# Splitting a transposing DMA into four pieces, one for each pair of heads, in a fused attention and bilinear-FFN kernel

## The chip, the cores and the metric

The kernel runs on one core of one Trainium2 chip. Times are device microseconds for one execution of the whole program; the median of several runs is quoted. Ratios are the mean time of one kernel's fast runs over the mean of the other's fast runs that are listed with it, so they are not quite the ratio of the medians. (Of the six runs of the kernel before that the changed kernel is set against, three are those that were known when the prediction was made.) All runs quoted as ratios were fast, that is, none was more than 1.5% above the fastest run of its kernel.

One core has several engines that work side by side: TensorE (PE) for matmuls, VectorE (DVE), ScalarE (ACT), GpSimd (POOL) and SyncE (SP). In this kernel POOL issues the DMAs that load and cast inputs, and SP issues stores and the transposing DMAs. The profile counts the packets of all of them together, on the core's 16 DMA engines.

## The reference, cut to what matters

```python
# batch, n_heads, seq, head_dim = 8, 8, 576, 64; d_model 512, d_ff 1536, 4608 tokens
kv  = np.einsum('bhsd,bhse->bhde', k, v)
out = np.einsum('bhsd,bhde->bhse', q, kv)
rms = np.sqrt(np.mean(out * out, axis=-1, keepdims=True) + 1e-06)
x   = (out / rms * g_norm)            # then to (tokens, d_model)
y   = ((x @ w_a) * (x @ w_b)) @ w_out
```

Almost all of the arithmetic is in the three FFN products. Attention is done batch by batch, just ahead of the FFN blocks that use it. Its matmuls want q with head_dim on the partitions, that is, transposed.

## The kernel before

The program is laid out by a small list scheduler in the kernel's own Python. Each piece of work is a node with an engine, a believed duration, a priority and its dependencies, each with a believed latency in microseconds. `plan.order()` runs through believed time and emits the instructions in the order that results. The beliefs are not waits: on the chip each engine takes its instructions in that fixed order, and semaphores hold it where the data isn't there. A wrong belief gives no wrong result; it gives an order in which an engine stands still.

Batches 0 and 1 are transposed on TensorE. From the third batch on, q is cast to bf16 into a scratch in DRAM and read back by a transposing DMA:

```python
def load_node(b, prio, dep, xt=None):          # dep: the load of the batch before
    ...
    def issue():                                # on POOL
        if dep is not None:
            # the gate: one element of the batch before's transposed q, copied to hold POOL
            nc.gpsimd.tensor_copy(gate_t, dep["q"].tile[0:1, 0, 0:1])
        ...
        for hl in range(2):                     # q -> scratch, cast to bf16
            nc.gpsimd.dma_start(out=scr[:, :, hl, :].rearrange("p s d -> s p d"), in_=qv[hl])
        ...                                     # then k in five DMAs, v in two
    def transpose():                            # on SP
        nc.sync.dma_start_transpose(
            out=ld["q"].tile[:].rearrange("p a s -> p (a s)"),
            in_=scr[:].rearrange("a s h d -> (a s) (h d)"),
        )
    ...
    ld["n"]  = plan.add("POOL", issue_us, prio, issue, ([(dep["qn"], 8.0)] if dep else []) + ..., ...)
    ld["qn"] = plan.add("SP", 2.5, prio, transpose, [(ld["n"], q_us)], [ld["q"]])
```

The load of the output weights (`wo_t`) stands behind the same kind of gate, on batch 2's q, and ahead of batch 3's load:

```python
def load_wo(dep):
    def issue():
        nc.gpsimd.tensor_copy(gate_t, dep["q"].tile[0:1, 0, 0:1])
        for i in range(2):
            sl = slice(i * FC // 2, (i + 1) * FC // 2)
            nc.gpsimd.dma_start(out=wo_t[:, sl, :], in_=wo_v[:, sl, :])
    return plan.add("POOL", 1.8, 50.0, issue, [(dep["qn"], 8.0)])
```

The first block's output product (L943 in the profile) reads `wo_t`; the scheduler believes that its halves are there 5.8 and 10.6 us after that issue:

```python
# in o_std
n1 = plan.add("PE", mm_us(OP, d_model), pr + 0.01 * f0, mm,
     [(wo_n, 5.8 if f0 + OP <= FC // 2 else 10.6), n1] + ..., ...)
```

Lines to know in the profile: L839 and L1008 are the FFN products, L943 the first block's output product, L624 the k·v product of a batch, L353 and L539 the readers of transposed q, L701 and L656 the gates, L704 the load of wo.

## Time and profile before

| | before |
|---|---|
| median time, 6 runs | 297.49 us (296.86 to 298.25) |
| span of the profiled run | 294.8 us |
| TensorE busy | 288.1 us, 98% |
| batch 2's transpose: starts, issued in, landed | 41.98, 6.49, 51.88 us |
| gate opens, wo issued | 51.94, 52.56 and 53.38 us |
| wo halves landed | 60.67 and 64.66 us |
| first L943 | 60.94 us |

Most of the lines behind this table stand in the prediction below. The "chain" of a page is the work that ended last, followed back step by step to what released it; its shares say what each step was, not what it cost. Read a timeline row as start, duration, engine, line, operation, output and inputs, count. "SPq" and "POOLq" rows are queues of these engines.

### The profile page before, as it was taken

The page shows a single profiled execution, that of the slowest core. Times are in us where ns is not written, and L with a number is a line of the kernel's source. Part 1 is how long each engine was busy: PE and PEld are TensorE (multiplying, and loading weights), DVE is VectorE, ACT ScalarE, POOL GpSimd, SP SyncE. Part 2 cuts the span into 40 slices and gives each one's busy share as a digit, 9 for nine tenths or more (in the row PEclk, how much of TensorE's full clock was granted, in tenths as well). Part 3 has the DMA queues.
Part 4 walks back from the last instruction along what each step waited for, and adds up shares of the span by engine and source line. Part 5 has one row for each costly group of instructions (what it writes and reads, how often), then busy time and mean ns, then how long its engine had stood idle before and what let it go on. Part 6 is the DMA issues. An engine that isn't in the chain of part 4 may idle for free.

```text
span 294.8 us, 6757 instructions
## 1 busy us (share of the span) xinstructions
PE 288.1 (98%) x2646; PEld 238.1 (81%) x2648; DVE 240.2 (81%) x441; ACT 191.7 (65%) x395; POOL 77.1 (26%) x96
## 2 busy tenths in 40 slices
PE   8999999999999999999999999999999999999993
PEld 3645558965888988899988998898988888888882
DVE  5454879893987988789979999979989958788852
ACT  3757667876578677877757866786769546665420
POOL 8945830950092470380001910000000000000000
PEclk9999999999999999999999999999999999999999
DMA  8999999699999999499816999330155001200053
GB/s 181 198 199 200 196 158 166 102 168 183 189 128 171 143 170 173 48 136 210 174 31 149 145 166 167 80 145 21 38 85 165 2 0 43 102 2 0 9 172 107
DMA packets 112643, 36.26 MB, mean 123 GB/s; under 512 B 89060, under 2 KB 108516, under 8 KB 112612
## 3 DMA queue, kind: packets, MB, share of 16 engines
q0 software_dynamic: 77552, 18.44, 65.9%
q1 hardware_dynamic: 34448, 16.70, 26.8%
q10 hardware_dynamic: 612, 0.71, 0.8%
q8 instruction: 20, 0.33, 0.5%
q14 instruction: 11, 0.09, 0.1%
HBM read 37.75 MB, written 14.75 MB: 178 GB/s over the span
## 4 chain that ended last, share of the span: by engine, by line
PE 93%; DVE 4%; issue 1%; ACT 1%; DVEq 0%; ACTq 0%
PE bk L839 47%; PE bk L1008 24%; PE bk L387 7%; PE bk L310 3%; PE bk L943 3%; PE bk L624 2%; PE bk L353 2%; PE bk L367 2%; PE bk L341 1%; PE bk L539 1%; PE bk L325 1%; DVE c L858 1%; DVE so L746 1%; DVE o_sb L1046 1%; DVE T L806 1%
## 5 line engine op out<-in xcount | busy, mean ns | idle before, releaser
L858 DVE TENSOR_TENSOR c<-bk,u 128x512 f16<-128x512 f32 x144 | 96.1, 684 | 19.3 <-PE bk L839 11.8
L420 ACT COPY u<-bk 128x512 f32<-128x512 f32 x144 | 81.4, 591 | 36.5 <-PE bk L839 29.9
L839 PE MATMUL bk<-xp,wa_t 128*128 128x256 f16 x288 | 55.0, 273 | 0.1
L839 PE MATMUL bk<-xp,wb_t 128*128 128x256 f16 x288 | 55.0, 273 | 0.0
L839 PEld LDWEIGHTS <-wa_t 128*128 128x128 f16 x384 | 37.1, 98 | 5.7 <-issue 0.3
L1008 PEld LDWEIGHTS <-abt 128*128 128x128 f16 x384 | 37.5, 98 | 4.7 <-issue 0.3
L839 PEld LDWEIGHTS <-wb_t 128*128 128x128 f16 x384 | 37.6, 98 | 4.4
L1008 PE MATMUL bk<-wo_t,abt 128*128 128x256 f16 x288 | 37.2, 273 | 0.1
L839 PE MATMUL bk<-T,sb 128*128 128x256 f16 x192 | 36.7, 273 | 0.0
L839 PE MATMUL bk<-T,sa 128*128 128x256 f16 x192 | 36.7, 272 | 0.0
L420 ACT CAST c<-bk 128x512 f16<-128x512 f32 x48 | 28.0, 587 | 12.1 <-PE bk L839 11.5
L893 DVE TENSOR_TENSOR abt<-c 128x1024 f16<-128x1024 f16 x48 | 32.7, 684 | 0.9
L839 PEld LDWEIGHTS <-sb 128*128 128x128 f16 x288 | 28.2, 98 | 3.3
L839 PEld LDWEIGHTS <-sa 128*128 128x128 f16 x288 | 27.9, 98 | 3.5
L1008 PEld LDWEIGHTS <-as 128*128 128x128 f16 x288 | 28.1, 98 | 3.3
L1040 ACT COPY o_sb<-bk 128x512 f32<-128x512 f32 x31 | 18.2, 586 | 18.5 <-PE bk L1008 18.0
L376 DVE SCALAR_TENSOR_TENSOR xp<-bk,g_col,rs 128x288 f16<-128x288 f32 x40 | 20.2, 512 | 10.9 <-ACT rs L371 10.9
L1008 PE MATMUL bk<-so,as 128*128 128x256 f16 x192 | 25.2, 273 | 0.0
L371 ACT ACTIVATE rs<-bk,eps_t 128x288 f32<-128x288 f32 x40 | 20.0, 506 | 6.2 <-PE bk L367 6.1
L667 POOL DMA_DIRECT2D k_t<-in_k_dram x24 | 21.2, 899 | 0.8 <-issue 0.5
L661 POOL DMA_DIRECT2D scr<-in_q_dram x12 | 19.6, 1638 | 2.5 <-issue 1.5
L1046 DVE TENSOR_TENSOR o_sb<-bk,o_sb 128x512 f32<-128x512 f32 (+1 forms) x25 | 16.4, 663 | 3.0 <-PE bk L1008 2.3
(107 smaller groups left out, 428.8 us busy)
## 6 DMA issues: line engine op xcount, KB each, us to landing
out_dram<-o_sb SPq DMA_DIRECT2D x20, 256.0 KB, 2.7
scr<-in_q_dram POOLq DMA_DIRECT2D x12, 288.0 KB, 8.0
k_t<-in_k_dram POOLq DMA_DIRECT2D x24, 128.0 KB, 8.2
v_t<-in_v_dram POOLq DMA_DIRECT2D x6, 512.0 KB, 11.0
out_dram<-o_sb SPq DMA_DIRECT2D x18, 128.0 KB, 2.4
wa_t<-in_moe_w_a_dram POOLq DMA_DIRECT2D x6, 256.0 KB, 10.6
wb_t<-in_moe_w_b_dram POOLq DMA_DIRECT2D x6, 256.0 KB, 10.8
wo_t<-in_moe_w_out_dram POOLq DMA_DIRECT2D x2, 768.0 KB, 9.7
```

Of the source, the lines that this page charges most:

```text
L371: nc.scalar.activation(rs, self.s_ps[p, h][:, 0:HF], AF.Abs_reciprocal_sqrt, bias=eps_t)
L376: nc.vector.scalar_tensor_tensor(out=xcols(p, self.b * S + h * HF, HF), in0=self.x_ps[p, h][:, 0:HF], scalar=g_col, in1=self.rs[p, h], op0 ...
L387: nc.tensor.matmul(ps[:, 0:n], lhsT=w[:, kc, fc * 128 : (fc + 1) * 128], rhs=xcols(kc, 0, n), start=(kc == 0), stop=(kc == KC - 1),)
L420: ("ACT", act_us(n), lambda: nc.scalar.copy(*args())),
L661: nc.gpsimd.dma_start(out=scr[:, :, hl, :].rearrange("p s d -> s p d"), in_=qv[hl])
L667: nc.gpsimd.dma_start(out=kt[:, c], in_=ks[:, :, c, :])
L839: nc.tensor.matmul(ps.tile[:, i * n : (i + 1) * n], lhsT=lhs(w, sm)[:, kc, :], rhs=rhs()[:, kc, :], start=start and i == 0 and kc == 0, st ...
L858: lambda: nc.vector.tensor_add(cs(fi, h), full(ps), u.tile),
L893: nc.vector.tensor_mul(t, c[:, :, :, 0], c[:, :, :, 1])
L1008: nc.tensor.matmul(ps.tile[:, sub * EH : (sub + 1) * EH], lhsT=lhs(slice(j, j + 1))[:, 0, sub * 128 : (sub + 1) * 128], rhs=rhs[:, j, :], ...
L1040: lambda: nc.scalar.copy(o(fi, h), bank(X, every)), [dep], takes, frees,
L1046: nc.vector.tensor_add(o(fi, h, subs), bank(ps, subs), other)
```

## The change

The intent: pieces can be issued and read one at a time, and pieces of the same shape, which the kernel already uses for x, land in 2.7 us. So the transposed q should be complete earlier, readers of the first heads could start earlier still, and the gate of the next loads could open earlier. The believed figures go along: 5.0 us of SP and 2.5 us to the landing, 7.5 in all, in place of 2.5 and 8.0.

```diff
-            return token_tiles(at, (w0 + 0.12 * (w1 - w0), w1), [m, (load["qn"], 8.0)])
-        slices(at, (w0 + 0.12 * (w1 - w0), w1), lambda p: [m, (load["qn"], 8.0)])
+            return token_tiles(at, (w0 + 0.12 * (w1 - w0), w1), [m, (load["qn"], 2.5)])
+        slices(at, (w0 + 0.12 * (w1 - w0), w1), lambda p: [m, (load["qn"], 2.5)])
@@ load_node
-                nc.gpsimd.tensor_copy(gate_t, dep["q"].tile[0:1, 0, 0:1])
+                nc.gpsimd.tensor_copy(gate_t, dep["q"].tile[0:1, NP - 1, 0:1])
@@ transpose
-            nc.sync.dma_start_transpose(
-                out=ld["q"].tile[:].rearrange("p a s -> p (a s)"),
-                in_=scr[:].rearrange("a s h d -> (a s) (h d)"),
-            )
+            for p in range(NP):
+                nc.sync.dma_start_transpose(
+                    out=ld["q"].tile[:, p, :], in_=scr[p].rearrange("s h d -> s (h d)")
+                )
@@ the plan's figures
-  "POOL", issue_us, prio, issue, ([(dep["qn"], 8.0)] if dep else []) + ...
+  "POOL", issue_us, prio, issue, ([(dep["qn"], 2.5)] if dep else []) + ...
-  "SP", 2.5, prio, transpose, [(ld["n"], q_us)], [ld["q"]]
+  "SP", 5.0, prio, transpose, [(ld["n"], q_us)], [ld["q"]]
@@ load_wo: the same gate and the same figure
-            nc.gpsimd.tensor_copy(gate_t, dep["q"].tile[0:1, 0, 0:1])
+            nc.gpsimd.tensor_copy(gate_t, dep["q"].tile[0:1, NP - 1, 0:1])
-        return plan.add("POOL", 1.8, 50.0, issue, [(dep["qn"], 8.0)])
+        return plan.add("POOL", 1.8, 50.0, issue, [(dep["qn"], 2.5)])
```

So there are two changes in one: a change of the transfer, and a change of what the scheduler believes about it. The second reorders instructions on TensorE, DVE, ACT and SP.

More of the change, by code (lines that the diff above doesn't have):

```diff
@@ L681, in transpose @@
         def transpose():
-            nc.sync.dma_start_transpose(
-                out=ld["q"].tile[:].rearrange("p a s -> p (a s)"),
-                in_=scr[:].rearrange("a s h d -> (a s) (h d)"),
-            )
+            for p in range(NP):
+                nc.sync.dma_start_transpose(
+                    out=ld["q"].tile[:, p, :], in_=scr[p].rearrange("s h d -> s (h d)")
+                )
         issue_us, q_us, ld["kv_us"] = (15.4, 4.3, 13.0) if dep is None else (9.0, 5.0 if b == 3 else 1.8, 16.0 if b == 3 else 13.0)
         ld["n"] = plan.add(
-            "POOL", issue_us, prio, issue, ([(dep["qn"], 8.0)] if dep else []) + ([(xt, TURN)] if xt else []), [ld["k"], ld["v"]]
+            "POOL", issue_us, prio, issue, ([(dep["qn"], 2.5)] if dep else []) + ([(xt, TURN)] if xt else []), [ld["k"], ld["v"]]
         )
         ld["qn"] = plan.add(
-            "SP", 2.5, prio, transpose, [(ld["n"], q_us)], [ld["q"]]
+            "SP", 5.0, prio, transpose, [(ld["n"], q_us)], [ld["q"]]
         )
```

## The prediction

> **What bounds the kernel now.** I read the page first, then TensorE's waits, then the chain that ended last.
>
> ```profile
> PE 288.1 (98%) x2646; PEld 238.1 (81%) x2648; DVE 240.2 (81%) x441; ACT 191.7 (65%) x395; POOL 77.1 (26%) x96
> PE 93%; DVE 4%; issue 1%; ACT 1%; DVEq 0%; ACTq 0%
> PE bk L310 <- DVE eps_t L274: 1.2, 1, 1.2
> 198.00 3.93 PE bk L839 x36
> ```
>
> The first two lines are the page's busy times and its chain by engine, the third is the longest of TensorE's own waits, the fourth a stretch of the chain. TensorE is busy for 98% of the span and its only wait of note is 1.2 us at the start. "Busy" could still hide stalls, because matmul ends are modelled, so I looked at starts: 36 matmuls of 256 columns take 3.93 us, 109 ns each, and nearly the whole trace from 25 us on has that spacing. I found two exceptions near 0.3 us. One is at 81 us, in TensorE's timeline:
>
> ```profile
> 80.33 0.38 PE L839 MATMUL bk<-T,wa_t 128*128 128x256 f16 x2
> 80.55 0.38 PE L839 MATMUL bk<-T,wb_t 128*128 128x256 f16 x2
> 81.03 1.47 PE L1008 MATMUL bk<-wo_t,abt 128*128 128x256 f16 x12
> ```
>
> Pairs should step by 0.22 us; the last step is 0.48, so 0.26 us is lost, while DVE finishes its sums. The other, of like size, is near 226 us. So the most that any reordering of loads can give here is about half a microsecond. What it can cost is not limited: TensorE takes its instructions in an order fixed at build time, and a late load stops it outright.
>
> Then the path that the change touches, from the q loads' view (first pair), the view of the same kind of transfer in four pieces that the kernel already has for x (second pair), and SyncE's and GpSimd's timelines:
>
> ```profile
> L682 SPq DMA_TRANSPOSE qT<-scr x6: 5981/6398/6860, 42.0 to 171.8; - x6
> DMA to landing us min/median/max: 9.9/10.3/11.9
> ...
> L594 SPq DMA_TRANSPOSE xp<-xs x12: 1152/1254/2024, 153.4 to 219.4; - x12
> DMA to landing us min/median/max: 2.6/2.7/4.1
> ...
> 41.98 6.49 SPq L682 DMA_TRANSPOSE qT<-scr  x1
> 153.36 5.95 SPq L594 DMA_TRANSPOSE xp<-xs  x4
> 184.94 5.10 SPq L594 DMA_TRANSPOSE xp<-xs  x4
> ...
> 51.94 0.68 POOL L701 COPY gate_t<-qT 1x1 bf16<-1x1 bf16 x1 [11.00 <-DMA qT<-scr]
> 52.56 1.64 POOL L704 DMA_DIRECT2D wo_t<-in_moe_w_out_dram  x2
> ```
>
> One transpose occupies SyncE 6.4 us and lands 9.9 to 11.9 us after it begins. GpSimd sits 11 us at a one-element copy that is there to wait for it, and only then issues the load of the output weights (wo), and after it batch 3. That gate is what the change moves.
>
> **What the Trainium skill says.** "TensorE: Matmul & The Clock Gate", section "Wait — 56ns, not 53.3ns?", gives N / 2.4 GHz + about 2.5 ns between warm matmuls, 109.2 ns at N = 256; the trace agrees (109 ns), which is why I call TensorE full. "DMA: Bandwidth & Descriptors", section "Issuing engines are not separate DMA queues", says that DMAs of all issuing engines run on the same 16 engines and interleave; section "Queues, rings and completion order" of the same page says that each engine goes round-robin between the queues with work, packet by packet. So a transpose cut into pieces is not free of the casting loads beside it. The windows view bears on that:
>
> ```profile
> 42.00:52.00 10.00, 10.00 (x94) 8.52 (x93) 10.00 (x22) 6.80 (x13) 0.06 (x1) 1.00 1.57 157
> 153.00:160.00 7.00, 7.00 (x66) 6.27 (x65) 5.56 (x10) 4.33 (x9) 0.00 (x0) 1.00 0.47 84
> 184.00:191.00 7.00, 7.00 (x67) 6.29 (x65) 6.59 (x13) 4.72 (x9) 0.00 (x0) 1.00 0.39 85
> ```
>
> The last two columns are the DMA share and GB/s. The pieces that land in 2.7 us ran when the DMA share was 0.39 to 0.47; the q transpose of batch 2 runs at 1.57, with batch 2's own k and v in flight.
>
> **The change, part by part.**
>
> *Issue.* Six instructions of 6.4 us become 24 of about 1.25 us, 5.1 to 5.95 us a batch: SyncE gains 0.5 to 1.3 us a batch. SyncE is not on the chain, so this counts only through the landing.
>
> *Landing of the last piece.* Let G be how much earlier the gate opens for batch 2. Before, 3.4 us pass between the end of the issue and the landing (9.9 - 6.49). The quiet pieces need 2.7 - 1.25 = 1.45 us. If the new pieces behave like quiet ones, they land 6.6 to 7.4 us after the start and G = 2.5 to 3.3 us. If the 3.4 us stays, because it is the crowd on the DMA engines that makes it, they land 8.5 to 9.35 us after the start and G = 0.6 to 1.4 us. I choose G = 1.0, since the crowd is the same in both kernels.
>
> *The order.* The program's list scheduler now believes in 5.0 + 2.5 = 7.5 us where it had 2.5 + 8.0 = 10.5, so it sets everything behind the gate 3.0 us earlier. The instruction orders show no matmul added or removed, and from batch 4's k·v product on, the same matmul count lies ahead of it in both. Between 51 and 103 us the order changes. I counted the matmuls from batch 2's k·v product (L624, starting at 51.35 us in the timeline) with the trace's spacings (109 ns for 256 columns, 216 for 512, 122 or 123 for 288, 56 for 128):
>
> - the first matmul on wo's first half is 7.71 us behind it, at 59.06 us (before: 60.94, and the count gives 60.93, so the method holds);
> - the first on wo's second half is 11.11 us behind it, at 62.46 us (before: 15.51 - 1.42 = 14.09 us behind, at 65.4);
> - batch 3's k·v product is 25.87 us behind it, at 77.22 us (before: 79.19; the trace has 79.21).
>
> *What these need.* The two wo loads are in this row of the load's view, minimum for the first half, maximum for the second:
>
> ```profile
> L704 POOL DMA_DIRECT2D wo_t<-in_moe_w_out_dram x2: 825/826/828, 52.6 to 53.4; - x2
> DMA to landing us min/median/max: 8.1/9.7/11.3
> ```
>
> First half: 52.56 + 8.1 = 60.66, so TensorE is on time at 59.06 if G is at least 1.60. Second half: 53.38 + 11.3 = 64.68, on time at 62.46 if G is at least 2.22. Batch 3's last v piece was issued at 67.14 and took 12.0 us in that window, 79.14, so G of 1.92 is wanted for 77.22; a stall at wo covers that one. Hence the stall is the larger of 0 and 2.22 - G, and it is paid once: what follows moves with it. With G = 1.0 that is 1.2 us.
>
> *What is won.* The 0.26 us at 81 us should go, since DVE has the time there in the new order (its sums move earlier, or TensorE waits at wo meanwhile). Batch 4 has about 2 us (last v piece issued at 89.30, 11.1 us by the median of its kind, against its k·v product at 102.80) and batches 5 to 7 have more, so an earlier load wins nothing there, and the tail after the last matmul (289.8 to 294.8 us) is untouched.
>
> *Sum.* 297.67 + 1.2 - 0.3 = 298.6 us at G = 1.0.
>
> **The rivals.**
>
> *Quiet landing.* The pieces land as those of x do, G is near 3, nothing stalls, and only the 0.26 us is won: about 297.4. For it: twelve pieces of the same shape at a median of 2.7 us, and early pieces can begin to move while later ones are issued. Against it: the DMA share of 1.57. I give it three chances in ten.
>
> *A worse landing.* Four transfers take turns with the loads and the last lands no earlier or later (G from -0.5 to 0). Then the stall is 2.2 to 2.7 us, plus perhaps half a microsecond if k and v of batch 2, which are wanted at 51.35, are pushed back by pieces that start sooner: 299.6 to 300.5. For it: transposes of this trace end only about a microsecond after the loads beside them. Against it: SyncE's issue itself ends sooner.
>
> *Transfer hidden anyway.* If slack at wo were larger than I read, the time would not move: 297.7. The row above leaves only 0.3 us for the first half in the kernel before (60.66 against 60.94), so I don't believe it.
>
> **Range and chances.** Seven parts of 298.6 and three of 297.4 give 298.2, a little more for the worse landing: 298.3. The three runs before spread over 1.4 us, so the range is 297.1 to 299.8. A gain of 2% would be 6 us, and there is not one of TensorE's time to win: 0.01. A loss of 6 us needs a stall at several batches: 0.03. Within 2%: 0.96.
>
> **What would show it right or wrong.** Four L683 transposes per batch of 1.2 to 1.6 us; for batch 2, the gate copy at about 51 us in place of 51.94 (near 49 under the first rival, 52 or later under the second). TensorE's starts should show one gap, of about 1.2 us, ahead of L943 between 59 and 63 us, and its new wait in the waits view on wo's DMA; the gap at 81 us should be gone and the order from batch 4 on be unmoved. I am wrong if the gate opens before 49.7 us, if L943 starts without a gap while the gate is late, or if new gaps stand at batches 3 to 7, which the count of slack says have none.

## The result, and the profile after

The changed kernel took 298.87 us (median of 6 runs, 298.49 to 299.21) against 297.49 us. The ratio is 1.0046, with a 95% interval of 1.0027 to 1.0065: slower, by 0.8 to 1.9 us, and inside 2%.

The page after, its busy times and its chain by engine; then the longest entry of TensorE's waits:

```profile
PE 287.5 (97%) x2648; PEld 237.8 (80%) x2648; DVE 240.5 (81%) x441; ACT 191.5 (65%) x395; POOL 77.4 (26%) x96
PE 75%; DMA 16%; POOL 4%; SPq 1%; DVE 1%; issue 1%; ACT 0%; DVEq 0%; ACTq 0%; POOLq 0%
PE bk L943 <- DMA wo_t<-in_moe_w_out_dram: 1.6, 1, 1.6
```

Where the chain was 93% TensorE, 16% of it is now DMA and 4% POOL. (This is not a loss of 20%: the chain now leads back from the wait at wo's second half through the loads of the first 65 us, and TensorE worked beside most of them. What the wait cost is read from TensorE's starts below.) A new wait stands in TensorE's list, on the load of wo. The chain from the 40th to the 62nd microsecond says why wo is late (columns: start, duration, what):

```profile
30.82 11.13 DMA scr<-in_q_dram
...
42.03 1.21 SPq L683
...
43.29 1.71 SPq L683
...
45.05 1.26 SPq L683
...
46.35 5.88 DMA qT<-scr
...
52.28 0.70 POOL gate_t L701
52.98 0.76 POOL wo_t L704
53.74 11.17 DMA wo_t<-in_moe_w_out_dram
```

Batch 2's q reaches the scratch at 41.95 us. The four pieces are issued one behind another, the last one lands at 52.23, POOL's gate opens, wo is issued, and its halves land at 61.20 and 64.91. From the first piece's start to the last landing it is 10.2 us, where the whole transpose needed 9.9. The gate opened at 52.28 us, 0.34 later than before. (In this trace batch 2's k·v product, too, starts 0.36 us later than before, so against TensorE's work the gate opened at about the same place.)

All pieces together, in the view of their line, with the time from issue to landing of a single piece:

```profile
L683 SPq DMA_TRANSPOSE qT<-scr x24: 1127/1354/2994, 42.0 to 178.3; - x24
DMA to landing us min/median/max: 5.3/7.6/8.6
```

A single piece took 7.6 us at the median from its own issue, where those of x took 2.7. The scheduler had been given 5.0 us of SyncE and 2.5 from there to the landing, 7.5 in all; for batch 2 it was 6.94 and 3.27, 10.2 in all. The windows view has the same crowd as before around batch 2's pieces (last two columns, DMA share and GB/s; the share sums the times of packets that overlap, so it can pass 1):

```profile
42.00:52.00 10.00, 10.00 (x90) 8.31 (x88) 10.00 (x21) 6.44 (x13) 0.00 (x0) 1.00 1.64 159
```

TensorE's timeline where it first reads wo, before:

```profile
60.72 0.38 PE L839 MATMUL bk<-T,sb 128*128 128x256 f16 x2
60.94 1.46 PE L943 MATMUL bk<-wo_t,abt 128*128 128x512 f16 x6
```

After, at both halves of wo, and at the place where the old order lost 0.26 us:

```profile
59.21 0.38 PE L839 MATMUL bk<-xp,sb 128*128 128x256 f16 x2
61.25 0.59 PE L943 MATMUL bk<-wo_t,abt 128*128 128x512 f16 x2 [1.65 <-DMA wo_t<-in_moe_w_out_dram]
...
64.42 0.38 PE L839 MATMUL bk<-xp,sb 128*128 128x256 f16 x2
64.95 1.24 PE L943 MATMUL bk<-wo_t,abt 128*128 128x512 f16 x5
...
81.05 0.38 PE L839 MATMUL bk<-T,sb 128*128 128x256 f16 x2
81.27 0.82 PE L1008 MATMUL bk<-wo_t,abt 128*128 128x256 f16 x6
```

A pair of L839 should be followed after 0.22 us, as it was before (60.94 - 60.72). The steps are 2.04 and 0.53, so 1.82 us are lost at wo's first half and 0.31 at its second, 2.13 us in all. (The 1.65 in brackets is less than the step, because the modelled end of the matmul before reaches into the gap.) The step at 81 us is 0.22: the 0.26 us of the old order are won. The balance of the trace is 2.13 - 0.26 = 1.87 us. The two profiled runs differ by 2.05 us (298.99 against 296.94); about 0.35 us of that is already there at batch 2's k·v product, 51.71 against 51.35 us, ahead of anything that the change touches. The six runs of each give 1.38 us between the medians, so the trace's balance lies near the upper end of the interval.

### The profile page after: what moved, and what is told of

Its sections match the earlier page's. It is cut to its first block, busy times and chain, and to the rows that moved or that the text cites. A ratio compares the mean times of both kernels' runs of the same rounds, so it can differ in the third digit from the quotient of the medians.

```text
span 296.8 us, 6790 instructions
## 1 busy us (share of the span) xinstructions
PE 287.5 (97%) x2648; PEld 237.8 (80%) x2648; DVE 240.5 (81%) x441; ACT 191.5 (65%) x395; POOL 77.4 (26%) x96
## 4 chain that ended last, share of the span: by engine, by line
PE 75%; DMA 16%; POOL 4%; SPq 1%; DVE 1%; issue 1%; ACT 0%; DVEq 0%; ACTq 0%; POOLq 0%
PE bk L839 44%; PE bk L1008 24%; DMA wb_t<-in_moe_w_b_dram 6%; DMA wo_t<-in_moe_w_out_dram 4%; DMA scr<-in_q_dram 4%; PE bk L943 3%; DMA qT<-scr 2%; PE bk L624 2%; SPq L683 1%; POOL as L242 1%; PE bk L539 1%; PE bk L367 1%; PE bk L353 1%; POOL so L242 1%; POOL scr L661 1%
## 5 line engine op out<-in xcount | busy, mean ns | idle before, releaser
L839 PE MATMUL bk<-xp,wa_t 128*128 128x256 f16 x288 | 54.9, 273 | 0.1
L839 PE MATMUL bk<-xp,wb_t 128*128 128x256 f16 x288 | 55.0, 273 | 0.0
L839 PEld LDWEIGHTS <-wa_t 128*128 128x128 f16 x384 | 37.1, 98 | 5.8 <-issue 0.3
L839 PEld LDWEIGHTS <-wb_t 128*128 128x128 f16 x384 | 37.6, 98 | 4.4
L839 PE MATMUL bk<-T,sb 128*128 128x256 f16 x192 | 36.6, 273 | 0.0
L839 PE MATMUL bk<-T,sa 128*128 128x256 f16 x192 | 36.6, 273 | 0.0
L839 PEld LDWEIGHTS <-sb 128*128 128x128 f16 x288 | 28.2, 98 | 3.3
L839 PEld LDWEIGHTS <-sa 128*128 128x128 f16 x288 | 27.9, 98 | 3.5
```

The source lines that it names most:

```text
L839: nc.tensor.matmul(ps.tile[:, i * n : (i + 1) * n], lhsT=lhs(w, sm)[:, kc, :], rhs=rhs()[:, kc, :], start=start and i == 0 and kc == 0, st ...
```

## The experiments

The change has two parts, so the first two runs take them apart. They were run with three and four below, 5 rounds each, against the same 11 runs of the kernel before (median 297.06 us).

**1. The pieces with the old figures.**

```diff
-  [m, (load["qn"], 2.5)]      (dep["qn"], 2.5)      "SP", 5.0
+  [m, (load["qn"], 8.0)]      (dep["qn"], 8.0)      "SP", 2.5
```

(Against the changed kernel; the lines are cut to the figures, in this diff and the next.)

> The four pieces, with the scheduler's old figures (2.5 us of SyncE and 8.0 us to the landing). The orders on TensorE, DVE, ACT and GpSimd are those of the kernel before, instruction for instruction; only the transposes differ. Theory A (the loss is the order that the new figures make, and the pieces land no earlier than the whole transpose): the ratio to before is 1.000 within 0.002, no gap ahead of L943, batch 2's gate copy at 51.7 to 52.4 us. Rival B (the pieces themselves cost the 1.4 us, through SyncE or the DMA engines): ratio 1.003 to 1.006.

Measured: 296.58 us, ratio 0.9986 (0.9974 to 0.9997). TensorE's timeline has no gap at wo, and the one at 81 us is back (starts at 80.62 and 81.10). The gate, in POOL's timeline:

```profile
52.12 0.56 POOL L701 COPY gate_t<-qT 1x1 bf16<-1x1 bf16 x1 [10.89 <-DMA qT<-scr]
```

The pieces do not open the gate earlier, and they cost nothing: the interval ends just under 1.000 (experiment 8 repeats this run). Theory A.

**2. The whole transpose with the new figures.**

```diff
-  [m, (load["qn"], 8.0)]      (dep["qn"], 8.0)      "SP", 2.5
+  [m, (load["qn"], 2.5)]      (dep["qn"], 2.5)      "SP", 5.0
```

(Against the kernel before.)

> The one transpose of before, with the scheduler's new figures (5.0 us and 2.5 us). The orders on TensorE, DVE, ACT and GpSimd are those of the changed kernel. Theory A: the whole loss is here too, ratio 1.004 to 1.006, with a gap of 1.5 to 2.1 us ahead of the first L943. Rival B: ratio 1.000 within 0.002.

Measured: 298.44 us, ratio 1.0054 (1.0037 to 1.0071). TensorE's timeline at wo:

```profile
59.09 0.38 PE L839 MATMUL bk<-xp,sb 128*128 128x256 f16 x2
61.16 0.59 PE L943 MATMUL bk<-wo_t,abt 128*128 128x512 f16 x2 [1.69 <-DMA wo_t<-in_moe_w_out_dram]
```

A step of 2.07 us in place of 0.22: the same stall without a single piece. So the figures carry the whole loss, and the pieces none of it. (Its profiled run, the slowest of its six, has one more gap, of 1.2 us at 196 us, where ACT waited for x's transposes; I have not followed that up. The median does not rest on that run; without it the ratio of the means is 1.0045.)

**3. The changed kernel, told that wo lands later.**

```diff
-  [(wo_n, 5.8 if f0 + OP <= FC // 2 else 10.6), n1]
+  [(wo_n, 8.3 if f0 + OP <= FC // 2 else 13.1), n1]
```

> The changed kernel, but the scheduler is told that the two halves of wo land 2.5 us later than it believed, so their first matmuls stand 9.14 and 13.22 us behind batch 2's k.v product and batch 3's k.v product 25.22. Theory A (every order that trusts the early gate pays somewhere): the gap ahead of L943 shrinks to 0 to 0.5 us, but batch 3's k.v product then comes at about 77 us, before its v (78.8 to 79.5 us), and waits 1.3 to 2.2 us; ratio 1.003 to 1.006. Rival C (only the wait at wo costs anything): the gap goes and the ratio is 0.999 to 1.001.

Measured: 297.45 us, ratio 1.0022 (1.0004 to 1.0040), between the theories. The profiled run was the fastest of its six (296.97 us, the slowest 299.10). Its TensorE timeline at wo, and batch 3's k·v product:

```profile
60.16 0.38 PE L839 MATMUL bk<-xp,wb_t 128*128 128x256 f16 x2
60.59 1.47 PE L943 MATMUL bk<-wo_t,abt 128*128 128x512 f16 x6
...
77.00 1.28 PE L624 MATMUL bk<-v_t,k_t 128*128 128x128 bf16 x20
```

The gap at wo is down to 0.21 us, as expected. But the wait that I expected at L624 is not there in this trace. The last v piece of batch 3 landed at 76.86 us, 10.1 us after its issue, where I had reckoned with 12. My second claim, that every order that trusts the early gate must pay elsewhere, is not shown. What is shown is less: in the profiled run mending the wait at wo leaves 0.21 us of the stall, but over all six runs the ratio falls only from 1.0046 to 1.0022, about half, and the two intervals overlap. Whether v is sometimes late in the slower runs of this kernel stays open: they have no trace.

**4. The changed kernel, with the gates on the first piece.**

```diff
-  nc.gpsimd.tensor_copy(gate_t, dep["q"].tile[0:1, NP - 1, 0:1])
+  nc.gpsimd.tensor_copy(gate_t, dep["q"].tile[0:1, 0, 0:1])
```

(In both places; the gate only sets the time of the next loads, and the readers of q wait for their own pieces.)

> The changed kernel with the gates on the first piece instead of the last. The first piece of batch 2 landed at 50.0 us in the changed kernel's trace, the last at 52.2. Theory A: the gate opens at 50.0 to 50.3 us, wo lands 2 us earlier, the gap ahead of L943 falls to 0 to 0.4 us and the ratio to before is 0.998 to 1.001. Rival D (loads let in 2 us earlier slow the last pieces or themselves by as much): the gap stays over 1 us and the ratio over 1.003.

Measured: 296.99 us, ratio 0.9996 (0.9984 to 1.0008). The gate in POOL's timeline and TensorE at wo:

```profile
49.45 0.18 POOL L701 COPY gate_t<-qT 1x1 bf16<-1x1 bf16 x1 [8.53 <-DMA qT<-scr]
...
58.97 0.38 PE L839 MATMUL bk<-xp,sb 128*128 128x256 f16 x2
59.19 0.59 PE L943 MATMUL bk<-wo_t,abt 128*128 128x512 f16 x2
```

The first piece landed at 49.40 us, the last at 51.75. The gate opens 2.5 us earlier than before, nearly what the scheduler believes, and the stall is gone to the last hundredth (a step of 0.22). The order of the changed kernel is thus sound; it was the gate that did not keep the promise. With no gap at 81 us either, the trace has some 0.26 us less of TensorE gaps than before, which five rounds cannot tell from nothing.

**5 and 6. The transfer by itself, with quiet DMA engines.** Within each batch's load, k and v are issued ahead of q, so that q's transpose starts when that batch's own loads are through and the next ones are still held by the gate. Once with the pieces (on the changed kernel), once with the whole transpose (on the kernel before). These are measuring kernels, one look each.

```diff
 def issue():
     ... gate
-    q -> scratch, two DMAs
     k, five DMAs; v, two DMAs
+    q -> scratch, two DMAs
```

> A measurement of the disputed cost, not a candidate: the changed kernel, with each batch's k and v issued ahead of its q, so that the q transposes begin when that batch's own k and v have landed and the next batch's wait at the gate. Theory A (the crowd on the DMA engines makes the landing late): from the first piece's start to the last piece's landing 6.0 to 7.5 us in batch 2 (10.2 with the crowd), each piece landing in 2.5 to 3.5 us, so the scheduler's 7.5 us is about right for quiet DMA engines. Rival E (four back-to-back q pieces are slow in themselves, for instance by how they read the scratch): 9 us or more here too. The kernel itself is late, 299 to 306 us, since the gates open later.

> The same with the kernel before's one transpose. Theory A: quiet, the whole transpose lands 6.5 to 8.5 us after its start (9.9 with the crowd), so that splitting it would gain only some 0 to 1.5 us even then, since what counts is the last row and the issue takes 5 to 6 us either way. Rival F (the whole transpose is slow by itself and the pieces would bring the 3 us once they run quiet): 9.5 us or more here, against 6.0 to 7.5 in the kernel with pieces.

Measured, pieces first and the whole transpose second, in the views of their lines:

```profile
L683 SPq DMA_TRANSPOSE qT<-scr x24: 1137/1210/1977, 49.2 to 197.0; - x24
DMA to landing us min/median/max: 2.5/2.7/4.6
```

```profile
L682 SPq DMA_TRANSPOSE qT<-scr x6: 1920/2037/2724, 49.1 to 180.4; - x6
DMA to landing us min/median/max: 4.3/4.6/5.8
```

Read the first pair for one piece and the second for all of q. Batch 2's four pieces were issued from 49.16 us on, in 5.13 us, and the last landed at 57.16: 8.0 us. The whole transpose was issued in 2.01 us and landed 4.27 us after its start. Both of my theories for the whole one were wrong (6.5 to 8.5, and 9.5 or more): at 4.3 us it was well below both. The first three pieces landed in 2.5 to 2.8 us each, as expected, but the last one took 4.1, so their 8.0 us is outside theory A's 6.0 to 7.5 as well. The crowd is confirmed as the cause of the late landing of the whole transpose (9.9 us with it, 4.3 without). And splitting does not shorten the transfer in either state: 10.2 against 9.9 us with the crowd, 8.0 against 4.3 without. The other batches agree: with k and v ahead, the pieces needed 6.4 to 8.0 us from first start to last landing, the whole transpose 4.3 to 5.8 (five landings).

The times of these two, 317.75 and 299.04 us, are those of single runs. Their orders were not made for such late gates; the one with pieces lost 5.8 us at wo alone, and more at later batches, with the granted clock at 0.973.

**7 and 8. Is there something better than both?** Seven is experiment 1 with the gates on the first piece; eight is experiment 1 once more. 5 rounds each, against 11 runs of the kernel before (297.05 us).

```diff
 # 7, against experiment 1
-  nc.gpsimd.tensor_copy(gate_t, dep["q"].tile[0:1, NP - 1, 0:1])
+  nc.gpsimd.tensor_copy(gate_t, dep["q"].tile[0:1, 0, 0:1])
```

> The four pieces, the scheduler's old figures (so the compute order of the kernel before) and the gates on the first piece: the most slack that these parts give. Theory A (TensorE is full, so slack at wo is worth nothing beyond the lost stall): wo lands about 2 us earlier than before, no gap ahead of L943, the 0.26 us gap at 81 us stays because it is DVE's, ratio 0.998 to 1.001. Rival (earlier loads do help somewhere): ratio under 0.997.

> The first experiment once more, to see whether its 0.9986 is a gain of the pieces or the scatter between calls. Theory A: its compute order and TensorE gaps are those of before, so the ratio is 1.000 within 0.0015 this time. Rival (the pieces themselves win 0.4 us): 0.9986 within 0.001 again.

Measured: 296.86 us, ratio 0.9998 (0.9981 to 1.0015), and 296.70 us, ratio 0.9991 (0.9976 to 1.0005). In seven the halves of wo landed at 58.34 and 63.17 us, more than 1 us before the kernel before had them, and the time did not move: slack at wo buys nothing. Eight leaves it open whether the pieces by themselves win 0.1%; its interval holds both 1.000 and the first result. Only experiment 1's interval lies under 1.000, and its repeat's does not, so no version tried here is shown to be faster than the kernel before.

## Why the prediction was right or wrong

The time was inside the range (298.87 in 297.1 to 299.8), with the right sign and the right place. The size of one term was off. That the time fell inside says little about that term: the range was set as wide as the scatter of three runs, and by the prediction's own sum it holds the time for any G from 0 (299.6 us) to 3 (297.4 us).

- **TensorE is full, so at most half a microsecond can be won.** Right. The one gap that the new order could close was closed (0.26 us), and four versions without the stall (experiments 1, 4, 7 and 8) all lie within 0.15% of the kernel before.
- **The count of matmuls to wo.** Right. 7.71 us behind batch 2's k·v product at 51.71 us is 59.42 us, and TensorE was there: the pair before L943 starts at 59.21. The second half follows at 51.71 + 11.11 + 1.82 = 64.64, and had to wait for 64.91.
- **Issue: "SyncE gains 0.5 to 1.3 us a batch".** Wrong, and this is the step that failed. I took the 1.25 us of a quiet piece. With the crowd, the last piece of each batch took 2.2 to 3.0 us to issue, and batch 2's four took 6.94 us, against 6.49 for the whole. The other half of the sum held: from the end of the issue to the landing it was 52.23 - 48.96 = 3.27 us, where I kept 3.4. I overlooked a simpler reading. In the eight traces with the usual order of loads, batch 2's q landed 1.0 to 1.2 us after that batch's last v piece (which landed at 50.5 to 51.2 us), as four pieces or as one transfer. That would make the landing a matter of the loads beside it, whatever the issue takes; experiments 5 and 6 fit it, but no run moves v alone, so it is not shown. The prediction had it only as an argument for the second rival.
- **G = 1.0 us.** It was -0.3 us by the clock: the gate opened at 52.28 in place of 51.94, while the transposes began 0.05 us later. It is better called 0. Batch 2's k·v product came 0.36 us later as well, and in the traces with the usual order of loads and the gate on the end of q the gate opened at 52.08 to 52.28 us with pieces (four runs), at 51.94 and 52.22 with the whole transpose. The prediction's own formula, 2.22 - G, gives 2.22 us of stall for G = 0; the trace has 2.13, not 1.2. That is what I had as the second rival, a worse landing, and its 2.2 to 2.7 us of stall. Its time of 299.6 to 300.5 us, from 297.67, is a loss of 1.9 to 2.8 us; the trace's balance is 1.87, and the medians show 1.38. That rival's share in my weights was far too small.
- **"Quiet landing" as the first rival.** Wrong twice. The DMA engines were not quiet, and quiet pieces are not faster than a quiet whole transpose. I compared pieces without the crowd with a whole one in it; the like-for-like pairs are those of experiments 5 and 6.
- **Batch 3's v.** My estimate took the smaller of two latencies of that window (12.0 us) for the last v piece; it was 12.35, to 79.49 us, and the k·v product had started at 79.21. That can be, since the product takes the last rows of v last. The same latency was 10.1 to 12.3 us in the other traces with the usual order of loads. No conclusion rested on it but that of experiment 3, which missed.
- **No change from batch 4 on.** Right: beside wo, TensorE's list has only two new waits, of 0.6 and 0.5 us, both in the first 8 us of the program, ahead of anything that the change touches.

On the skill: the formula for the spacing of matmuls ("TensorE: Matmul & The Clock Gate", "Wait — 56ns, not 53.3ns?") agreed throughout, with 109 ns (the 109.2 ns that the prediction gives for 256 columns is worked out from it; the section prints no value for that size). That all DMAs interleave on the same 16 engines ("DMA: Bandwidth & Descriptors", "Issuing engines are not separate DMA queues") was the right warning, and experiment 6 puts a number to it: 5.6 us of the 9.9. That an engine takes turns between its queues packet by packet, which the prediction also cites, no run here tests.

## What to carry to other kernels

Where an instruction order is computed from believed durations, test the beliefs apart from the change that they describe: the pieces with the old figures and the old transfer with the new figures told in two runs where the loss came from. A DMA's latency belongs to the traffic around it, so a figure taken from a quiet stretch of the same trace must not be carried into a crowded one. And splitting a transfer helps those that wait for its first part; a gate on the last part gets nothing from it.

## What the Trainium skill lacked or had wrong

- "DMA: Bandwidth & Descriptors", section "DMA Transpose (X-bar)", gives no cost on the issuing queue for a transposing DMA of these sizes. Here a 128x576 piece held SyncE for 1.2 us and a 128x2304 one for 2.0 us with quiet DMA engines, so four pieces cost 5.1 us for what one does in 2.0.
- The same page has no figure for a transpose beside a full stream of casting loads. Here the landing went from 4.3-5.8 us to 9.9-11.9 us, and SyncE's own row for it from 2.0 to 6.4 us, so the row's length in such a stretch is not the work of issuing alone. Its section "Latency and other measured facts" has the first byte of a hardware-generated DMA at about 600 ns; with the crowd, the packet records show batch 2's first transposed packet about 4.2 us after the start of the issue, in both kernels, and 1.3 us after it in experiments 5 and 6, without the crowd.
